# Turning 1/std and a few constants with VectorE and ScalarE instead of TensorE at the start of a layernorm + gated-MLP + state-space kernel

## The chip, the cores and the metric

One core of one Trainium2 chip runs the whole program. The metric is the device time of one execution in microseconds (us). Each profile belongs to one execution and has its own span. The span is about 2 us shorter than the time (before: 502.6 and 504.46 in the profiled execution). A run is in a slow state when its granted TensorE clock is low; that happened once here, to a run of the kernel before (522.75 us at clock 0.949), and that run is in no number below.

## The reference, cut to what matters

```python
# x: 1 x 2048 x 576 in bf16; w_gate, w_up: 576 x 4608; w_down: 4608 x 576
x  = A_x
xn = (x - mean(x)) / sqrt(var(x) + 1e-5)                 # row by row
glu = (sigmoid(xn @ w_gate) * (xn @ w_up)) @ w_down
y   = state_space(xn, Lambda, B, C, log_dt) + xn * Dskip   # a scan over the 2048 rows
out = x + y + glu
```

The kernel takes the rows in blocks of 512. Only the start of the first block matters here. To let TensorE start early, the first ten groups of gate and up columns are multiplied with x that is centred but not yet divided by its standard deviation. Each result is scaled by 1/std afterwards. The matmul leaves the rows of x along the columns of PSUM, while 1/std is computed with one row per partition. So 1/std (4 columns of 128 partitions) must be spread: every partition needs all 512 values along its columns, as the tile `scale0`.

## The kernel before: the parts that the change and the argument touch

```python
class RawGateUp(GateUp):                   # one group of 128 gate and up columns, 512 rows
    def evac(self):
        gu = consts.tile([P, 2, TB], FP32, name="gu", tag=("T2", "C2", "S2")[self.f % 3])
        nc.vector.tensor_mul(gu[:], self.ps[:], scale0[:].unsqueeze(1).to_broadcast([P, 2, TB]))  # VectorE
        sT = evp.tile([P, TB], BF16, name="sT")
        nc.scalar.activation(sT[:], gu[:, 0, :], ACT.Sigmoid)                                     # ScalarE
        h = hpool.tile([P, TB], BF16, name="hT", bufs=2 * FC)
        nc.gpsimd.tensor_mul(h[:], sT[:], gu[:, 1, :])                                            # GpSimd
# ... cut ...
def ln_norm(tt):                           # the next block's first two row tiles, on VectorE
    for dst, src in XN_PARTS:
        nc.vector.tensor_scalar(xn[:, dst], xts[tt][:, src], mvs[nb][:, tl, 0:1], rstds[nb][:, tl:tl + 1],
                                ALU.subtract, ALU.mult)
# ... cut: the start ...
consts_transpose(ptrs[0][:, 0:P])          # two TensorE transposes of 27 rows of constants
ln_log(rstds[0][:], ssq[:, 0:TT_B], 1.0 / D)
ln_exp(0)                                  # 1/std of the first block, on ScalarE
consts_copy(ptrs[0][:, 0:P])               # three ScalarE copies
exp_first()
for tt in range(TT_B, 2 * TT_B - 1):
    ln_stats(tt)                           # VectorE statistics of the next block
for t in range(2):                         # matmuls of the first two groups, rows 256 to 511
    for g in start_groups:
        # ...
        g.turn(t, slice(2 * P, TB))
spread = ptrs[1][:].bitcast(FP32)
for tt in range(TT_B):                     # four TensorE transposes of a broadcast column
    over_rows(spread[:, tt * P:(tt + 1) * P], rstds[0][:, tt:tt + 1])
nc.scalar.copy(scale0[:], spread)
# ... means, squares and 1/std of the next block, load of the sigmoid table (ScalarE) ...
third = RawGateUp(0, 2, 0)
# ...
for g in start_groups:
    g.evac()
```

`gu` has three buffers, so the fourth `gu` waits for the first product on GpSimd. The groups share four PSUM pairs (`pgu`), so a group's first matmul waits for the `gu` of the group four places ahead. A group's stretch of matmuls is called its turn below.

## Time and profile before

| | before |
|---|---|
| time, median of 3 | 504.34 us (504.28 to 504.44) |
| span of the profiled run | 502.6 us |
| TensorE busy | 498.2 us (99%) |
| VectorE, ScalarE, GpSimd busy | 327.0, 213.7, 101.0 us |

### The profile page before, as it was taken

How to read it: one execution, taken by the hardware profiler on the slowest of the kernel's cores; microseconds unless marked ns; L12 is line 12 of the kernel's file. 1: busy time of each engine (PE TensorE's matmuls, PEld its weight loads, DVE VectorE, ACT ScalarE, POOL GpSimd, SP SyncE). 2: the span in 40 equal slices, each digit the busy share in tenths (PEclk: the TensorE clock that was granted, in tenths of full speed). 3: DMA queues.
4: the chain of work that ended last, by engine and by line, in shares of the span. 5: the costliest groups of instructions: out<-in, count | busy, mean ns of one | idle time of the engine just before them, and what ended most of it. 6: DMA issues, size and time to landing. Idle time of an engine off the chain costs nothing.

```text
span 502.6 us, 13289 instructions
## 1 busy us (share of the span) xinstructions
PE 498.2 (99%) x5819; PEld 287.9 (57%) x5819; DVE 327.0 (65%) x717; ACT 213.7 (43%) x395; POOL 101.0 (20%) x140
## 2 busy tenths in 40 slices
PE   8999999999999999999999999999999999999997
PEld 5444675444576444577655445764445774446775
DVE  6969799787794777868769766947666842221112
ACT  6965692555501755610152564015565005553000
POOL 8576100223100133110001332000431101300000
PEclk9999999999999999999999999999999999999999
DMA  9948530244443194221302541100641100500001
GB/s 260 170 103 256 142 58 27 66 137 132 90 103 84 22 262 120 64 76 36 69 2 90 161 132 43 44 25 1 202 121 54 44 26 14 188 1 3 25 26 47
DMA packets 38347, 44.32 MB, mean 88 GB/s; under 512 B 25298, under 2 KB 30866, under 8 KB 38290
## 3 DMA queue, kind: packets, MB, share of 16 engines
q0 software_dynamic: 9424, 32.57, 21.7%
q1 hardware_dynamic: 27906, 10.41, 10.0%
q8 instruction: 45, 0.74, 0.6%
q10 hardware_dynamic: 960, 0.51, 0.4%
q14 instruction: 12, 0.10, 0.1%
HBM read 35.54 MB, written 2.36 MB: 75 GB/s over the span
## 4 chain that ended last, share of the span: by engine, by line
PE 98%; DMA 1%; DVE 0%; issue 0%
PE pgu L565 56%; PE pd L739 33%; PE pbu L565 7%; PE pd L699 1%; PE pd L707 1%; DMA xt<-in_A_x_dram 1%; PE ptr L923 0%; DVE xn L287 0%; DVE xn L933 0%; PE ptr L926 0%; DVE xT L938 0%; DVE ob L708 0%; PE ptr L234 0%
## 5 line engine op out<-in xcount | busy, mean ns | idle before, releaser
L565 PE MATMUL pgu<-xT,wgu 64*128 64x512 bf16 (+1 forms) x2190 | 276.7, 373 | 0.4 <-DVE xT L938 0.4
L565 PEld LDWEIGHTS <-wgu 64*128 64x128 bf16 x2190 | 113.1, 94 | 131.8 <-issue 0.7
L600 ACT ACTIVATE sT<-pgu 128x512 bf16<-128x512 f32 x134 | 80.1, 598 | 159.0 <-PE pgu L565 158.9
L739 PE MATMUL pd<-wd,hT 64*128 64x288 bf16 x2208 | 140.0, 283 | 0.0
L603 DVE TENSOR_TENSOR hT<-sT,uT 128x512 bf16<-128x512 bf16 x134 | 56.8, 424 | 117.7 <-ACT uT L601 117.4
L739 PEld LDWEIGHTS <-hT 64*128 64x128 bf16 x2208 | 107.5, 94 | 30.0
L565 PE MATMUL pgu<-xT,wrem 64*128 64x512 bf16 (+1 forms) x438 | 109.4, 373 | 0.0
L601 ACT CAST uT<-pgu 128x512 bf16<-128x512 f32 x134 | 77.8, 581 | 0.0
L168 POOL DMA_DIRECT2D wgu<-in_B_w_gate_dram x35 | 26.8, 766 | 227.5 <-PE pgu L565 226.1
L182 POOL DMA_DIRECT2D wd<-in_B_w_down_dram x36 | 25.5, 711 | 96.5 <-PE pd L739 96.0
L650 ACT COPY bure<-pbu 128x512 f32<-128x512 f32 x16 | 9.4, 587 | 74.7 <-PE pbu L565 73.9
L565 PEld LDWEIGHTS <-wrem 64*128 64x128 bf16 x438 | 28.0, 94 | 16.9
L757 DVE TENSOR_TENSOR acc<-acc,pd 128x576 f32<-128x576 f32 x36 | 25.4, 747 | 13.0 <-PE pd L739 13.0
L565 PE MATMUL pbu<-xT,bt 64*128 64x512 bf16 x240 | 31.8, 376 | 0.0
L739 PE MATMUL pd<-ctre,hst 64*128 64x288 bf16 x224 | 28.6, 283 | 0.0
L739 PE MATMUL pd<-ctim,hst 64*128 64x288 bf16 x224 | 28.6, 283 | 0.0
L739 PEld LDWEIGHTS <-hst 64*128 64x128 bf16 x504 | 24.5, 94 | 6.7
L168 POOL DMA_DIRECT2D wgu<-in_B_w_up_dram x35 | 26.2, 750 | 0.7 <-issue 0.6
L513 DVE TENSOR_TENSOR_SCAN gre<-r,g0re,wrim 128x512 bf16<-128x512 f32 x20 | 25.6, 1279 | 0.1
L754 DVE TENSOR_TENSOR ob<-acc,pd 128x576 bf16<-128x576 f32 x14 | 9.9, 750 | 23.2 <-PE pd L739 23.2
L565 PEld LDWEIGHTS <-bt 64*128 64x128 bf16 x240 | 12.4, 94 | 14.6
L520 DVE TENSOR_TENSOR_SCAN gim<-r,g0im,wrim 128x512 bf16<-128x512 f32 x16 | 20.3, 1266 | 0.0
(156 smaller groups left out, 369.7 us busy)
## 6 DMA issues: line engine op xcount, KB each, us to landing
wd<-in_B_w_down_dram POOLq DMA_DIRECT2D x36, 288.0 KB, 4.4
wgu<-in_B_w_gate_dram POOLq DMA_DIRECT2D x35, 256.0 KB, 3.5
wgu<-in_B_w_up_dram POOLq DMA_DIRECT2D x35, 256.0 KB, 4.0
out_dram<-ob SPq DMA_DIRECT2D x15, 144.0 KB, 1.8
wrem<-in_B_w_gate_dram POOLq DMA_DIRECT2D x5, 384.0 KB, 6.0
xt<-in_A_x_dram SPq DMA_DIRECT2D x13, 144.0 KB, 4.4
wrem<-in_B_w_up_dram POOLq DMA_DIRECT2D x5, 192.0 KB, 5.8
xt<-in_A_x_dram SPq DMA_DIRECT2D x4, 72.0 KB, 3.6
```

The costliest lines, as they stand in the source:

```text
L168: return [engs[gi].dma_start(w[:, gi, :, :], src[0:R0, fs].rearrange("(c p) f -> p c f", p=P)) for gi, src in enumerate((B_w_gate, B_w_up))]
L182: nc.gpsimd.dma_start(wd[:], B_w_down[f0:f0 + FP * P, :].rearrange("(n p) d -> p n d", p=P))
L513: nc.vector.tensor_tensor_scan(gre[:], r_bc, w[:, 0, :], g0re[:, col], ALU.mult, ALU.add)
L520: nc.vector.tensor_tensor_scan(gim[:], r_bc, w[:, 1, :], g0im[:, col], ALU.mult, ALU.add)
L565: m = nc.tensor.matmul(self.ps[:, which, cols], lhsT, rhs, start=start, stop=stop)
L600: nc.scalar.activation(sT[:], self.ps[:, 0, :], ACT.Sigmoid)
L601: nc.scalar.copy(uT[:], self.ps[:, 1, :])
L603: nc.vector.tensor_mul(h[:], sT[:], uT[:])
L650: nc.scalar.copy(bre[:], self.ps[:, 0, :])
L739: m = nc.tensor.matmul(pds[k][:, a, 0:DH], lhsT[rows, :], rhs[rows, a * DH:(a + 1) * DH], start=turn == 0 and i == 0, stop=turn == 1 and i ...
L754: nc.vector.tensor_add(halves(ob[:]), halves(acc[:]), pd[:, :, 0:DH])
L757: nc.vector.tensor_add(halves(acc[:]), halves(acc[:]), pd[:, :, 0:DH])
```

## The change

The intent is to take six small transposes off TensorE, which has no idle time. VectorE can transpose blocks of 32x32. A transpose of the four columns of 1/std, each broadcast over 32 columns, gives four tiles of 32 partitions (quarters), each right for its own quarter's rows. Each piece must then be copied to the other quarters. Four copies of a quarter go to VectorE and four to ScalarE, and then each engine does one copy of a half. The constants too go through VectorE's transpose, one 32x32 block into each quarter. The order changes with it: the spread sits behind two of the three statistics on VectorE, and the constants' copies sit behind the spread on ScalarE.

```diff
-    def consts_transpose(ps):
-        for half in (slice(0, H), slice(H, P)):
-            nc.tensor.transpose(ps[half, 0:3 * NH], crows[:], ident[0:3 * NH, 0:3 * NH])
+    def consts_transpose():
+        for q in range(4):
+            nc.vector.transpose(crowsT[q * Q:(q + 1) * Q, :], crows[:, q % 2 * Q:(q % 2 + 1) * Q])
 ... cut: consts_copy reads crowsT, crows is padded to 32 rows with zeros, ident32 goes ...
-    def over_rows(dst, col):
-        nc.tensor.transpose(dst, col.to_broadcast([P, P]), ident32[:])
+    def over_rows(dst, src):
+        blocks = ssmp.tile([P, TT_B, Q], FP32, name="blocks", tag="wrim", bufs=1)
+        nc.vector.transpose(blocks[:], src.unsqueeze(2).to_broadcast([P, TT_B, Q]))
+        dst = dst.rearrange("p (t q i) -> p t q i", t=TT_B, i=Q)
+        copies = (nc.vector.tensor_copy, nc.scalar.copy)
+        for i in range(2):
+            for side, copy in enumerate(copies):
+                for j in range(2):
+                    a, b = 2 * side + i, 2 * side + j
+                    copy(dst[b * Q:(b + 1) * Q, :, a, :], blocks[a * Q:(a + 1) * Q, :, :])
+        for side, copy in enumerate(copies):
+            a, b = side * H, (1 - side) * H
+            copy(dst[b:b + H, :, 2 * side:2 * side + 2, :], dst[a:a + H, :, 2 * side:2 * side + 2, :])
 ... cut ...
-    consts_transpose(ptrs[0][:, 0:P])
+    consts_transpose()
     ln_log(rstds[0][:], ssq[:, 0:TT_B], 1.0 / D)
     ln_exp(0)
-    consts_copy(ptrs[0][:, 0:P])
+    for tt in range(TT_B, 2 * TT_B - 2):
+        ln_stats(tt)
+    over_rows(scale0[:], rstds[0][:])
+    ln_stats(2 * TT_B - 2)
+    consts_copy()
     exp_first()
-    for tt in range(TT_B, 2 * TT_B - 1):
-        ln_stats(tt)
 ... cut: the matmuls of the first two groups, as before ...
-    for tt in range(TT_B):
-        over_rows(spread[:, tt * P:(tt + 1) * P], rstds[0][:, tt:tt + 1])
-    nc.scalar.copy(scale0[:], spread)
```

More of the change, by code (lines that the diff above doesn't have):

```diff
@@ L191 @@
     make_identity(nc, ident[:])
-    crows = consts.tile([3 * NH, H], BF16, name="crows")
+    Q = P // 4
+    crows = consts.tile([Q, H], BF16, name="crows")
+    nc.vector.memset(crows[:], 0.0)
     iota = ssmp.tile([P, TB], FP32, name="iota", tag="buim", bufs=2)
@@ L231, with consts_copy @@
     ldt, lre, lim = (cvals[:, i, :] for i in range(3))
-    def consts_transpose(ps):
-        for half in (slice(0, H), slice(H, P)):
-            nc.tensor.transpose(ps[half, 0:3 * NH], crows[:], ident[0:3 * NH, 0:3 * NH])
-    def consts_copy(ps):
-        rows = ps[:, 0:3 * NH].rearrange("p (i a) -> p i a", a=NH)
+    crowsT = consts.tile([P, Q], BF16, name="crowsT")
+    def consts_transpose():
+        for q in range(4):
+            nc.vector.transpose(crowsT[q * Q:(q + 1) * Q, :], crows[:, q % 2 * Q:(q % 2 + 1) * Q])
+    def consts_copy():
+        rows = crowsT[:, 0:3 * NH].rearrange("p (i a) -> p i a", a=NH)
         nc.scalar.copy(cvals[0:H, :, :], rows[0:H, :, 0:NH:2])
@@ L899 @@
     xT_tile(1)
-    ident32 = ssmp.tile([P, P], FP32, name="ident32", tag="wrim", bufs=1)
-    nc.vector.tensor_copy(ident32[:], ident[:])
     start_groups = [RawGateUp(0, f, 0) for f in range(2)]
@@ L968 @@
         rstds[nb] = lnp.tile([P, TT_B], FP32, name="rstd")
-    consts_transpose(ptrs[0][:, 0:P])
+    consts_transpose()
     ln_log(rstds[0][:], ssq[:, 0:TT_B], 1.0 / D)
     ln_exp(0)
-    consts_copy(ptrs[0][:, 0:P])
+    for tt in range(TT_B, 2 * TT_B - 2):
+        ln_stats(tt)
+    scale0 = hpool.tile([P, TB], FP32, name="scale0", tag="hst", bufs=10)
+    over_rows(scale0[:], rstds[0][:])
+    ln_stats(2 * TT_B - 2)
+    consts_copy()
     exp_first()
-    for tt in range(TT_B, 2 * TT_B - 1):
-        ln_stats(tt)
     for t in range(2):
@@ L980 @@
             g.turn(t, slice(2 * P, TB))
-    spread = ptrs[1][:].bitcast(FP32)
-    for tt in range(TT_B):
-        over_rows(spread[:, tt * P:(tt + 1) * P], rstds[0][:, tt:tt + 1])
-    scale0 = hpool.tile([P, TB], FP32, name="scale0", tag="hst", bufs=10)
-    nc.scalar.copy(scale0[:], spread)
     start_mean(2 * TT_B - 1, nc.scalar)
```

## The prediction

> **What bounds the kernel now.** I read the page's part 4 first, then the chain of waits in order of time, then the timeline of the first 36 us for one engine after another, because the diff touches only the start. Part 4 gives the whole chain to TensorE:
>
> ```profile
> PE 98%; DMA 1%; DVE 0%; issue 0%
> ```
>
> So a microsecond taken out of TensorE's own sequence is a microsecond of the result, and work on another engine costs nothing unless TensorE comes to wait for it. The chain in order of time shows the two pieces that the change removes, ptr L234 (constants turned) and ptr L926 (1/std spread); columns are start, length, what:
>
> ```profile
> 9.59 0.13 PE ptr L234 x2
> 9.72 2.07 PE pgu L565 x36
> 11.79 0.58 PE ptr L926 x4
> 12.37 41.98 PE pgu L565 x388
> ```
>
> They are 0.13 + 0.58 = 0.71 us on the path, with no gap around them: the next piece starts where the last ends. From 12.37 on TensorE runs without a wait, so what matters is by how much each matmul group could still afford a late operand. A group's PSUM pair comes free when VectorE has scaled the group four places earlier (gu, L615). VectorE, start and length:
>
> ```profile
> 9.08 0.49 DVE L938 COPY xT<-ptr 128x640 bf16<-128x640 bf16 x1 [0.35 <-PE ptr L923]
> 9.49 0.81 DVE L265 BATCH_NORM_STATS2 bnst<-xt 128x6 f32<-128x288 bf16 x2
> ...
> 11.39 0.77 DVE L265 BATCH_NORM_STATS2 bnst<-xt 128x6 f32<-128x288 bf16 x2
> ...
> 13.02 2.36 DVE L615 TENSOR_TENSOR gu<-pgu,scale 128x1024 f32<-128x1024 f32 x2 [0.62 <-ACT scale L985]
> ...
> 18.40 2.36 DVE L615 TENSOR_TENSOR gu<-pgu,scale 128x1024 f32<-128x1024 f32 x2 [0.40 <-POOL hT L619]
> ```
>
> ```profile
> 27.07 2.35 DVE L615 TENSOR_TENSOR gu<-pgu,scale 128x1024 f32<-128x1024 f32 x2
> ```
>
> and TensorE's two turns that need the first and the eighth of these:
>
> ```profile
> 15.33 1.03 PE L565 MATMUL pgu<-xT,wgu 64*128 64x512 bf16 x8
> ```
>
> ```profile
> 28.93 1.03 PE L565 MATMUL pgu<-xT,wgu 64*128 64x512 bf16 x8
> ```
>
> The reader is to see two things. VectorE is nearly full from 13 to 30.5 us (4.96 us busy of 5 in 20 to 25 and in 25 to 30, in the table by stretches), so a late start there isn't made up. And the slack is small: one gu takes 1.22 us, so the first is done at 13.02 + 1.22 = 14.24 and TensorE wants its PSUM at 15.33 (slack 1.09); the eighth is done at 27.07 + 1.22 = 28.29 and is wanted at 28.93 (slack 0.64). In between I count 1.2 (sixth group of that ring, 18.01 against 19.22), 1.0 (24.08 against 25.05) and more for the others. The tightest place is at 28.93.
>
> ScalarE and GpSimd close the loop, since gu has three buffers and the fourth gu waits for the first product on GpSimd:
>
> ```profile
> 12.40 0.58 ACT L985 COPY scale<-ptr 128x512 f32<-128x512 f32 x1 [0.65 <-PE ptr L926]
> 12.89 0.69 ACT L289 ACTIVATE xn<-xt 128x576 bf16<-128x576 bf16 x1
> ...
> 15.19 1.28 ACT L991 ACT_TABLE_LOAD   x1
> ...
> 16.49 1.15 ACT L617 ACTIVATE sT<-gu 128x512 bf16<-128x512 f32 x2
> ...
> 17.20 3.41 POOL L619 TENSOR_TENSOR hT<-sT,gu 128x512 bf16<-128x512 bf16 x3 [3.97 <-ACT sT L617]
> ```
>
> **What the Trainium skill says.** (1) "VectorE: DVE Perf Modes", section "The three transpose paths": VectorE turns 32x32 blocks only, and a 128x128 bf16 block set takes 311 ns. That is why copies between quarters are needed. The trace of before has no such instruction. (2) The same page, section "Two Vector instructions with no wait between them": an instruction that starts in another group of 32 partitions than the last read or write there starts only when all earlier ones are finished. The trace agrees where it can: memsets that stay at partition 0 overlap (0.81, 0.85, 0.87), the one that moves to partition 64 waits for the end of the one before (0.87 + 0.06 = 0.93, start at 0.97), and the one that moves back waits again (1.08):
>
> ```profile
> 0.85 0.06 DVE L222 MEMSET zero_t<- 128x1 f32 x1
> 0.87 0.06 DVE L244 MEMSET sg_pm<- 64x1 f32 x1
> 0.97 0.06 DVE L245 MEMSET sg_pm<- 64x1 f32 x1
> 1.08 0.06 DVE L481 MEMSET g0re<- 128x5 f32 x1
> ```
>
> (3) "ScalarE: Activation LUTs", section "What ACT_TABLE_LOAD costs": an ACTIVATE with immediate scale takes 186 ns + 0.833 ns per element, and back-to-back ones overlap by about 93 ns. The exp of 128x4 took 206 ns here, the formula gives 189: it agrees. (4) "Advanced Engine Details and Errata", section "VectorE Performance Modes": VectorE's second port is shared with GpSimd and they block each other. The trace shows it: a 128x64 product of VectorE (L343) that starts at 21.00 lasts 1.15 us, until the GpSimd product of 20.93 to 22.10 is over.
>
> **The change part by part.**
> Removed from TensorE: 0.71 us, as above. Removed from VectorE: the 0.56 us copy of the identity at 1.34, which lies in idle time (worth 0). Removed from ScalarE: the 0.58 us scale copy. The order of the built kernel shows that TensorE's remaining matmuls keep their order and that the third group then waits for weights alone. Those land at about 10 us (issued at 5.00, 5.0 us) and their remainder rows at 6.30 + 5.2 = 11.5, wanted at 11.66 + 0.86 = 12.5: no new wait for a DMA. The memset of the constants' rows and the waits of three small loads on it fall before 2 us (0).
>
> Added to VectorE, in its order. a) Four 32x32 transposes of the constants, ahead of the statistics, each into another quarter, so by (2) each held, and the statistics held behind them. With the skill's 311 ns for 128 columns, less 96 columns at 0.96 GHz, one is about 0.21 us (an estimate): 4 x 0.21 = 0.85, so the statistics start at 9.49 + 0.85 = 10.34. b) Two statistics as before, 11.39 - 9.49 = 1.90, plus the tail of 0.08: 12.3. 1/std itself is ready at 11.22 (exp, 11.02 + 0.20) and no longer waited for. c) The block transpose, 128 columns: 0.31, to 12.63. d) Four quarter copies of 128 elements, held one after another: about 0.22 us each (an estimate: 64 cycles at two elements a cycle and some 150 fixed, from the skill's page of (1)), 0.88, to 13.5; up to 0.2 more each while GpSimd writes descriptors until 13.23. e) One half copy of 256 elements, 0.29, to 13.8. f) The third statistics, 11.39 to 12.40 before, so 1.0: 14.8. Only then the first gu: 14.8 against 13.02, late by d0 = 1.8 us.
>
> Added to ScalarE: after the blocks at 12.63, four copies of 128 elements at 186 + 107 - 93 = 200 ns a step, the last in full, 0.89, then one of 256 elements that waits for them, 0.40: 13.97 with the hops. Behind it stand now the constants' copies and their exp, which took 11.76 - 11.13 = 0.63 before: 14.6. Only then comes the mean that began at 12.89: dA = 1.7 us late, and with it everything behind it: table load, first sT at 16.49 + 1.7 = 18.2, first hT done at 20.0, fourth gu at 20.1 against 18.40.
>
> So VectorE's delay is d0 = 1.8 for the first three gu and dA = 1.7 from the fourth on (0.4 us of VectorE idle before it is used up). What TensorE makes of it: each turn may start at its old time less 0.71, or when its PSUM is free. At 15.33: 14.24 + 1.8 = 16.04, which is 0.7 later than before. At 28.93: 28.29 + 1.7 + 0.05 for the semaphore = 30.0, which is 1.1 later than before. The largest of these counts, not their sum, since a turn once late is late for all that follow and the later slack grows by it. After 30.5 VectorE is idle for over a microsecond per group (1.69 us before the hT at 32.24), so nothing more is lost. Sum: -0.71 gained, then 1.8 us of waits, net +1.1 at most of the straight sum.
>
> **The rivals.** A. The straight gain: VectorE's small transposes and copies overlap, d0 about 0.8 and dA about 0.9; the waits shrink to about 1.0 and the net is about +0.3 (504.6). The full -0.71 (503.6) needs both delays under 0.0 to 0.4, which the block transpose behind two statistics nearly rules out: it can't start before 11.8. B. A relief by chance: the 128x64 product of (4) is blocked for 1.15 us because it comes 0.07 us after GpSimd's. If it slips ahead, VectorE gets back about 1.1 us before 28.93, and the turn at 15.33 or 19.22 decides: net +0.3 to +0.7 (504.6 to 505.0). C. Contention: descriptor writing holds the quarter copies, d0 grows to 2.3 or more; then the first gu decides, net +1.2 to +1.6 (505.5 to 505.9). D. The late normalised tiles: ScalarE's last of the next block was done at 20.34, its transposing DMA takes 3 to 4 us, wanted at 26.99; 1.7 us later it lands near 26: it speaks against a new wait there.
>
> **Range and chances.** The straight sum says 504.34 + 1.1 = 505.4, A and B lie 0.4 to 0.8 below it, C half a microsecond above; weighed together, 505.1. 8 times in 10 between 504.2 and 505.9. Two per cent would be 10 us, over ten times any term here: within 2% has 0.985, slower 0.01, faster 0.005.
>
> **What would show it.** TensorE without any ptr L234 or L926 piece, the third group at about 11.66; the first gu at about 14.8 and the fourth at 20.1; in the chain of waits, VectorE's gu appearing ahead of TensorE's turns near 16 and near 30, with idle time of TensorE of 1 to 2 us in the first 31 us that the page before doesn't have; after 31 us the same chain as before, shifted. Wrong would be: a first gu before 14 us, or TensorE with no idle behind gu (then the time is 503.6), or the table load not later than 15.9.

## The result, and the profile after

| | before | after |
|---|---|---|
| time, median of 6 | 504.31 us (504.05 to 504.99) | 505.77 us (505.6 to 506.17) |
| span of the profiled run | 502.6 us | 503.6 us |
| TensorE busy | 498.2 us | 497.7 us |
| VectorE busy | 327.0 us | 329.3 us |

The ratio after/before is 1.0028, with a 95% interval of 1.0016 to 1.0041. Such ratios, here and below, divide the mean time of one kernel's fast runs by that of the other's fast runs in the same rounds, so they are not quite the ratio of the medians quoted. The change is within 2%, and inside that it is a clear small loss: 0.28% of 504.3 is 1.4 us.

The share of the whole chain by engine, part 4 of the page of the kernel after, shows where the loss is: VectorE holds 3% of a chain that was TensorE's almost alone.

```profile
PE 96%; DVE 3%; DMA 1%; issue 0%; DVEq 0%
```

The chain of waits of the kernel after, in order of time (start, length, what), near the two turns that the prediction named:

```profile
13.88 0.83 DVE bnst L269 x2
...
14.86 1.19 DVE gu L619
16.05 0.04 issue
16.09 7.96 PE pgu L569 x72
...
28.67 1.23 DVE gu L619
29.90 0.04 issue
29.94 10.09 PE pgu L569 x91
```

No piece of a transpose of constants or of 1/std is on TensorE any more. Instead the first `gu` (14.86) stands ahead of the turn at 16.09, and the eighth `gu` (28.67) stands ahead of the turn at 29.94. TensorE's own list has the wait at the first of them in brackets:

```profile
16.09 1.04 PE L569 MATMUL pgu<-xT,wgu 64*128 64x512 bf16 x8 [1.66 <-DVE gu L619]
```

The bracket counts idle time from the modelled end of the matmul before. By TensorE's pace the turn is due 0.86 us after the last set of seven matmuls begins, which is at 13.38 here. So it was due at 14.24, and the wait is 1.85. VectorE's list of the kernel after, from the constants to the fourth `gu`:

```profile
9.12 0.84 DVE L238 STREAM_TRANSPOSE crowsT<-crows 32x32 bf16<-32x32 bf16 x4
...
11.88 0.26 DVE L929 STREAM_TRANSPOSE blocks<-rstd 128x128 f32<-128x128 f32 x1
12.18 1.36 DVE L936 COPY scale<-blocks 32x128 f32<-32x128 f32 x4
13.57 0.29 DVE L939 COPY scale<-scale 64x256 f32<-64x256 f32 x1
...
14.86 2.31 DVE L619 TENSOR_TENSOR gu<-pgu,scale 128x1024 f32<-128x1024 f32 x2
...
17.41 1.18 DVE L312 TENSOR_SCALAR xn<-xt,mv,rstd 128x512 bf16<-128x512 bf16 x4
...
19.99 2.36 DVE L619 TENSOR_TENSOR gu<-pgu,scale 128x1024 f32<-128x1024 f32 x2 [0.20 <-POOL hT L623]
```

And the chain of ScalarE and GpSimd beside it, that sets the fourth `gu`:

```profile
12.18 1.21 ACT L936 COPY scale<-blocks 32x128 f32<-32x128 f32 x4 [1.21 <-DVE blocks L929]
13.42 0.40 ACT L939 COPY scale<-scale 64x256 f32<-64x256 f32 x1
...
16.78 1.28 ACT L1002 ACT_TABLE_LOAD   x1
18.07 1.15 ACT L621 ACTIVATE sT<-gu 128x512 bf16<-128x512 f32 x2
```

```profile
18.79 3.42 POOL L623 TENSOR_TENSOR hT<-sT,gu 128x512 bf16<-128x512 bf16 x3 [5.28 <-ACT sT L621]
```

Laid beside the lines of the kernel before, the first `gu` is 1.84 us later (13.02 to 14.86). The table load is 1.59 later (15.19 to 16.78), and the fourth `gu` 1.59 later (18.40 to 19.99). The eighth is 1.60 later (27.07 to 28.67), and TensorE's turn behind it is 1.01 later (28.93 to 29.94). The spans differ by the same 1.0.

One correction belongs to this. In the run profiled after, the start itself was 0.36 us earlier than in the one profiled before: the last copy of the centred x begins at 8.72 and not at 9.08. This is no work of the change, as the kernels derived from before or after begin that copy anywhere from 8.58 to 9.08. Counted from that copy, the turn is 21.22 - 19.85 = 1.37 us late, which is the 1.4 of the mean times.

### The profile page after: what moved, and what is told of

The parts are those of the page before. It is cut to its first block, busy times and chain, and to the rows that moved or that the text cites.

```text
span 503.6 us, 13292 instructions
## 1 busy us (share of the span) xinstructions
PE 497.7 (99%) x5813; PEld 334.1 (66%) x5813; DVE 329.3 (65%) x727; ACT 214.8 (43%) x399; POOL 101.1 (20%) x140
## 4 chain that ended last, share of the span: by engine, by line
PE 96%; DVE 3%; DMA 1%; issue 0%; DVEq 0%
PE pgu L569 53%; PE pd L743 33%; PE pbu L569 7%; PE pd L703 1%; PE pd L711 1%; DVE gu L619 1%; DMA xt<-in_A_x_dram 1%; DVE bnst L269 0%; DVE scale L936 0%; DVE tmpxd L347 0%; PE ptr L925 0%; DVE crowsT L238 0%; DVE xn L291 0%; DVE xn L946 0%; DVE xT L951 0%
## 5 line engine op out<-in xcount | busy, mean ns | idle before, releaser
L569 PEld LDWEIGHTS <-wgu 64*128 64x128 bf16 x2190 | 130.0, 94 | 114.6 <-issue 2.9
L743 PEld LDWEIGHTS <-hT 64*128 64x128 bf16 x2208 | 125.9, 94 | 11.6
L569 PE MATMUL pgu<-xT,wrem 64*128 64x512 bf16 (+1 forms) x438 | 111.9, 373 | 0.0
L569 PEld LDWEIGHTS <-wrem 64*128 64x128 bf16 x438 | 30.4, 94 | 14.5
L743 PEld LDWEIGHTS <-hst 64*128 64x128 bf16 x504 | 28.7, 94 | 2.5
L569 PEld LDWEIGHTS <-bt 64*128 64x128 bf16 x240 | 14.3, 94 | 12.5
```

Of the source, the lines that this page charges most:

```text
L569: m = nc.tensor.matmul(self.ps[:, which, cols], lhsT, rhs, start=start, stop=stop)
L743: m = nc.tensor.matmul(pds[k][:, a, 0:DH], lhsT[rows, :], rhs[rows, a * DH:(a + 1) * DH], start=turn == 0 and i == 0, stop=turn == 1 and i ...
```

## The experiments

The theory is the prediction's: two delays (VectorE's own, and that of ScalarE and GpSimd) of which the larger decides at each of TensorE's turns. Its rivals are that the constants alone do it, that contention with GpSimd does it, or that the order of the instructions does it and not the work. The table gives every run. "Before" is the kernel before in the same rounds, on the same chip.

| kernel | median (lowest to highest), us | ratio to before, 95% | spans, us |
|---|---|---|---|
| 1 constants alone | 504.15 (504.11 to 504.37) | 0.9995 [0.9981, 1.0008] | 502.1 to 502.4 |
| 2 ScalarE's constants early | 507.12 (505.66 to 507.64) | 1.0046 [1.0032, 1.0060] | 503.7 to 505.7 |
| 3 statistics ahead | 506.57 (506.41 to 506.93) | 1.0043 [1.0031, 1.0056] | 504.4 to 504.9 |
| 4 spread alone | 505.74 (505.06 to 505.77) | 1.0023 [1.0010, 1.0035] | 503.1 to 503.8 |
| 5 = 4, product later | 504.61 (504.49 to 504.82) | 1.0005 [0.9991, 1.0019] | 502.4 to 502.7 |
| 6 = 2, product later | 505.46 (505.27 to 505.74) | 1.0022 [1.0009, 1.0035] | 503.2 to 503.7 |
| 7 quiet GpSimd | 505.65 (505.40 to 505.99) | 1.0026 [1.0011, 1.0040] | 503.3 to 503.9 |
| 8 one quarter (one run, state unknown) | 505.34 | none | 503.3 |
| 9 = 5 and 7 | 504.35 (504.28 to 505.47) | 1.0006 [0.9993, 1.0018] | 502.1 to 503.3 |
| 10 before, 4 needless statistics | 505.92 (505.15 to 506.92) | 1.0032 [1.0017, 1.0047] | 503.3 to 505.1 |
| 11 before, 6 needless statistics | 506.80 (506.26 to 506.95) | 1.0046 [1.0032, 1.0060] | 504.3 to 505.1 |
| 12 = 10, product later | 504.54 (504.10 to 505.16) | 1.0000 [0.9986, 1.0013] | 502.1 to 503.2 |

All were correct against the reference. For number 8, whose constants are wrong, that only shows that the tolerance doesn't notice them.

### 1. The constants alone

```diff
 (against before)
+    crows = consts.tile([Q, H], BF16, name="crows")      # and a memset
-    consts_transpose(ptrs[0][:, 0:P])     # TensorE
+    consts_transpose()                    # VectorE, four 32x32
 ... 1/std still spread by TensorE, order as before
```

> Only the constants go to VectorE; 1/std is spread by TensorE as before. Theory (a turn of TensorE waits for the latest of its inputs, the largest lateness counts): the four transposes put the first gu at about 13.3 us against 13.0, inside its slack of 1.1, ScalarE is not later; TensorE loses only its 0.13 us piece, so the span is 502.5 against 502.6 and the ratio to before 0.9995 to 1.0000. Rival (added VectorE work on the start's path costs its own length): the span grows by 0.86 - 0.13 = 0.7 to 503.3, ratio 1.0014.

Measured: 504.15, a tie with before (medians 504.15 and 504.45). TensorE has no wait, and the first `gu` starts at 12.99 although the statistics begin 0.84 us of transposes later: the delay is used up in VectorE's idle time ahead of the first `gu`. So alone this part is neither the loss nor much of a gain. With the spread behind it on VectorE that is no longer so: runs 5 and 6 compare the two.

### 2. ScalarE's copies of the constants ahead of the spread

```diff
 (against after)
     ln_exp(0)
+    consts_copy()
+    exp_first()
     for tt in range(TT_B, 2 * TT_B - 2):
 ...
     ln_stats(2 * TT_B - 2)
-    consts_copy()
-    exp_first()
```

> The changed kernel, but ScalarE does the constants' copies and their exp in its idle 1.2 us ahead of the spread instead of behind it. Theory: the first gu stays at 14.9 and the turn that waits for it at 16.1; the fourth gu comes 0.2 us earlier, the second wait (near 29.9) vanishes as its cause shrinks by up to 0.75; the end moves by the difference of the two latenesses alone, 0.25 us: span 503.35. Rival (ScalarE's chain alone carries the loss): span 603.6 - 0.75, that is 502.85, since the wait near 16 would be made up later. Rival (VectorE's chain alone): span unchanged at 503.6.

(The text has a slip: "603.6 - 0.75" should read 503.6 - 0.75.) This missed. It was not faster than the kernel after but slower and more scattered, with spans from 503.7 to 505.7. The profiled run, the fastest of the five, shows one reason in VectorE's list, where the bracket is a wait for a load of x:

```profile
10.69 0.82 DVE L269 BATCH_NORM_STATS2 bnst<-xt 128x6 f32<-128x288 bf16 x2 [0.35 <-DMA xt<-in_A_x_dram]
```

The start of that run is also 0.36 us later than in the kernel after (copy of centred x at 9.08), so that the first `gu` began at 15.19 and TensorE's turn at 16.42. Its span (503.7) is that of the kernel after. The second wait is gone, as expected (30.01 is 1.94 after the turn before it, the pace), but the late data and the later start hid the gain. The four slower runs have no trace. What they could be came out in run 4, and run 6 tested it. Run 4 shows a collision of VectorE's four normalising instructions with GpSimd's first product. In this profile the two already touch: the normalisation ends at 18.92, and the product starts at 18.86.

### 3. The third statistics ahead of the spread

```diff
 (against after)
-    for tt in range(TT_B, 2 * TT_B - 2):
+    for tt in range(TT_B, 2 * TT_B - 1):
         ln_stats(tt)
     scale0 = ...
     over_rows(scale0[:], rstds[0][:])
-    ln_stats(2 * TT_B - 2)
```

> The changed kernel with the third statistics ahead of the spread instead of behind it: the same VectorE work before the first gu, but ScalarE gets the blocks 0.93 us later. Theory: first gu still at 14.7 to 14.9 and its turn at about 16.0, but the table load, the first hT and the fourth gu 0.9 later, so the second wait grows to put that turn at 30.8 instead of 29.9: span 504.5. Rival (only the first gu counts): span 503.6, no change.

This run separates the two delays. VectorE reaches the first `gu` as early as in the kernel after (14.78, of which 0.40 us is a wait for ScalarE's half copy), but ScalarE's copies come 0.9 us later, and so do the table load (17.71 instead of 16.78) and the fourth `gu` (20.91 instead of 19.99). In TensorE's list:

```profile
16.05 1.04 PE L569 MATMUL pgu<-xT,wgu 64*128 64x512 bf16 x8 [1.63 <-DVE gu L619]
...
30.86 1.04 PE L569 MATMUL pgu<-xT,wgu 64*128 64x512 bf16 x8
```

The first turn is where it was (16.09 after), but the turn near 30 moved from 29.94 to 30.86, by 0.92 us, and the spans rose by 0.8. So ScalarE's delay decides at the late turn, as the prediction says, and the order of the spread in front of the third statistics is worth 0.9 us.

### 4. The spread alone

```diff
 (against the kernel of run 2)
-    consts_transpose()
+    consts_transpose(ptrs[0][:, 0:P])     # TensorE again, 0.13 us
```

> Only the spread goes to VectorE; the constants are turned by TensorE as before and copied by ScalarE in its idle time ahead of the spread. Theory: without the four transposes the first gu starts at about 14.0, its turn at 15.2 to 15.3 (15.33 before); ScalarE's mean begins near 12.95 (12.89 before), so no second wait: span 502.4 to 502.6, ratio 0.9995 to 1.0005. Rival (the spread's own 2 us on VectorE carry the loss, the constants are harmless): span 503.3 or more.

This missed too: 502.5 was expected, and 503.1 to 503.8 came, the number of the rival. Three engines of this run, VectorE, then GpSimd, then TensorE, show a cost that the prediction did not have:

```profile
16.98 2.02 DVE L309 TENSOR_SCALAR xn<-xt,mv,rstd 128x512 bf16<-128x512 bf16 x4
```

```profile
17.79 2.32 POOL L620 TENSOR_TENSOR hT<-sT,gu 128x512 bf16<-128x512 bf16 x2 [3.62 <-ACT sT L618]
```

```profile
20.27 1.04 PE L566 MATMUL pgu<-xT,wgu 64*128 64x512 bf16 x8 [0.54 <-DVE gu L616]
```

The four normalising instructions took 2.02 us instead of the 1.18 of both main kernels, and TensorE waited a second time, at 20.27. The last of the four starts at 17.85, 0.06 us after GpSimd's first product, and lasts 1.16 us, about as long as one product. In the kernel before, the normalisation is over at 16.80 and the first product starts at 17.20. In the kernel after, the figures are 18.59 and 18.79. Here ScalarE is only 0.58 us behind before (sT at 17.07), but VectorE is 1.4 behind (first `gu` at 14.43; 0.53 of it is a load of x that came late), so the product overtakes the normalisation. The Trainium skill has the reason, on "SBUF — State Buffer", section "Who interferes with whom": VectorE and GpSimd share one pair of ports, and the one that has it locks the other out. The 1.16 us agrees with it, and run 5 tests it.

### 5. Run 4 with GpSimd's first product behind the normalisation

```diff
 (against run 4)
         sT = ...; nc.scalar.activation(sT[:], gu[:, 0, :], ACT.Sigmoid)
+        if self.f >= 2: self.product()        # the first two products are issued later
 ...
     for _ in range(2):
         ln_norm(...); ln_dma_transpose(...)
+    for g in start_groups:
+        m = g.product()
+        tc.add_manual_dep(m.ins, last_norm[0].ins.name, PE_ORDER, reason="behind the normalisation")
```

> Only the spread on VectorE (as the run before of that kind, span 503.7 where 502.5 was expected), and GpSimd's first product waits until VectorE's four normalising instructions are done. In that earlier run they took 2.02 us instead of 1.18, as GpSimd's product began at 17.79 amid them, and a second wait of TensorE appeared at 20.27. Theory (ScalarE, now earlier, starts GpSimd inside VectorE's two-port work): the four take 1.2 us again, the wait at 20.3 is gone, only the one near 15.5 stays: span 502.6 to 503.1. Rival (the third gu is late for another cause): the span stays at 503.5 to 503.8.

As expected. VectorE, GpSimd and TensorE of this run:

```profile
16.26 1.18 DVE L311 TENSOR_SCALAR xn<-xt,mv,rstd 128x512 bf16<-128x512 bf16 x4
```

```profile
17.59 4.91 POOL L627 TENSOR_TENSOR hT<-sT,gu 128x512 bf16<-128x512 bf16 x4 [4.25 <-DVE nmr L319]
```

```profile
14.94 1.04 PE L568 MATMUL pgu<-xT,wgu 64*128 64x512 bf16 x8 [0.56 <-DVE gu L618]
```

The normalisation is back at 1.18 us, and the wait near 20 is gone. Counted by TensorE's pace, as for the kernel after, what stays is 0.75 us at 14.94 (the bracket says 0.56) and 0.22 us at 28.75, too short for a bracket, against the 0.58 us of transposes saved. All five spans (502.4 to 502.7) lie below all five of run 4, so it isn't the late load of run 4's profile alone. The time ties with before (504.61 against 504.27). So the spread on VectorE and ScalarE costs about what it saves, within that interval, once the collision is out of the way.

### 6. Run 2 with the same dependence

```diff
 (against run 2: the same edit as in run 5)
```

> ScalarE's constants ahead of the spread (whose runs spread from 503.7 to 505.7 in span) with the same dependence of GpSimd's first product. Theory (the slow ones of those runs are such collisions): all runs within 503.1 to 504.0 in span, median time near 505.5. Rival (the slow ones come from the next block's x landing late, 10.67 in the profiled run): the runs spread as before, up to 505 and more.

As expected: spans of 503.2 to 503.7 instead of 503.7 to 505.7. The scatter of run 2 went when the collision was ruled out. That its slow runs were collisions is therefore likely but not shown: no trace of one exists, and run 6 ran on another chip, where loads of x may have landed otherwise. TensorE's turn near 16 waited, and the one at 29.75 came 0.20 us behind the pace:

```profile
15.95 1.04 PE L571 MATMUL pgu<-xT,wgu 64*128 64x512 bf16 x8 [1.67 <-DVE gu L621]
```

At 505.46 it is 0.3 us below the kernel after (505.77), as expected, but the two intervals overlap widely.

Runs 5 and 6, in the same rounds, differ only in the engine that turns the constants. With VectorE (run 6) the kernel is 0.85 us slower (505.46 against 504.61, and the two sets of times don't overlap), its first `gu` starts at 14.72 instead of 13.71 and the turn behind it at 15.95 instead of 14.94. So the four transposes, free alone (run 1), cost about their own length once the spread stands behind them on VectorE.

### 7. GpSimd quiet during the copies

```diff
 (against after)
-        nc.gpsimd.dma_start(dskip_rows[:], ...)          # after the load of weights (0, 3)
-        load_wgu((0, 4))
+    def last_loads(behind):                              # called behind VectorE's half copy
+        load = nc.gpsimd.dma_start(dskip_rows[:], ...)
+        tc.add_manual_dep(load.ins, behind.ins.name, PE_ORDER, reason="behind the spread")
+        load_wgu((0, 4))
```

> The changed kernel, but GpSimd writes the descriptors of the last two loads of the start (0.55, 0.75 and 0.75 us from 11.45 to 13.5 in the changed kernel) only after VectorE's half copy. Theory: VectorE's four quarter copies take 0.9 us instead of 1.36, the first gu comes at about 14.4 instead of 14.86 and its turn at 15.6 instead of 16.1; but the second wait hangs on ScalarE's chain and stays at 29.9, so the span stays at 503.4 to 503.6. Rival (the copies are slow by themselves): four copies still 1.3 us or more.

This is rival C of the prediction taken alone. VectorE's copies, then TensorE's late turn, in this run:

```profile
12.11 0.90 DVE L939 COPY scale<-blocks 32x128 f32<-32x128 f32 x4
```

```profile
29.88 1.04 PE L572 MATMUL pgu<-xT,wgu 64*128 64x512 bf16 x8 [0.16 <-DVE gu L622]
```

The four copies took 0.90 us, not 1.36, so contention with GpSimd's descriptors was real and cost VectorE 0.46 us in the profiled run. It doesn't strike every time: in run 5 the four took 0.90 us too, though descriptors were being written beside them (11.30 to 12.59). The first `gu` came at 14.35 and the first turn at 15.58, half a microsecond earlier than after (14.86 and 16.09). Yet the turn near 30 is at 29.88 against 29.94, and the time is the same (505.65 against 505.77). The gain at the first turn was given back in two waits (by the pace 0.38 at 25.66 and 0.34 at 29.88, where the kernel after has none and 0.26), because ScalarE's chain, which the edit leaves alone, still sets the fourth `gu` (19.93, waiting 0.65 for GpSimd). This shows what bounds the changed kernel: VectorE's slow copies don't set its end.

### 8. The four constants' transposes into one quarter

```diff
 (against after; the constants come out wrong, on purpose)
-            nc.vector.transpose(crowsT[q * Q:(q + 1) * Q, :], crows[:, ...])
+            nc.vector.transpose(crowsT[0:Q, q * Q:(q + 1) * Q], crows[:, ...])
```

> The changed kernel with the four 32x32 transposes of the constants all written into the first quarter of the partitions, beside one another (wrong constants on purpose). If each is held because it writes to another quarter than the one before: the four take 0.3 to 0.4 us instead of 0.84. If a transpose takes 0.2 us anyway: 0.84 as before.

In VectorE's list:

```profile
9.29 0.47 DVE L239 STREAM_TRANSPOSE crowsT<-crows 32x32 bf16<-32x32 bf16 x4
```

The same four instructions that all start in the first quarter take 0.47 us instead of 0.84, and the statistics behind them start 0.40 us after the first of them instead of 0.86. This is the rule from which the prediction took its 0.85: an instruction that moves to another quarter is held until the ones ahead are done.

### 9. Both cures together

```diff
 (run 5 and the edit of run 7)
```

> The spread alone on VectorE, GpSimd's first product behind the normalisation, and GpSimd's last descriptors behind the spread: the best version that the runs so far point to. In the earlier run of the first two (span 502.4) the half copy took 0.54 us under GpSimd's descriptors and the turn near 14.9 waited 0.56. Theory: half copy 0.29, that wait 0.2 to 0.4, no second wait, span 502.0 to 502.3, ratio to before 0.9990 to 1.0000. Rival: a wait near 18.5 takes its place, span 502.4 or more.

This is the best version with the spread off TensorE. The half copy took 0.29 us and the first wait is 0.34 by its bracket, as expected. By the pace TensorE waits 0.50 us at 14.64 and 0.21 at 28.45, for 0.58 us saved. Three of the five spans lie in the expected 502.0 to 502.3. Its profiled span of 502.1 equals the fastest of before, but its five runs reach up to 503.3, and the median ties with before: 504.35 against 504.34. So nothing here beats the kernel before; it only takes back the loss of the kernel after.

### 10 and 11. The kernel before with VectorE delayed

```diff
 (against before, 4 in run 10, 6 in run 11)
+    idle = consts.tile([P, 4, BN], FP32, name="idle")
+    for i in range(4):
+        nc.vector.bn_stats(idle[:, i, :], xts[0][:, 0:DH])    # read by nobody
     spread = ptrs[1][:].bitcast(FP32)
```

These delay VectorE alone, without the change, to see whether its slack of 1.09 us at 15.33 is what the prediction says.

> The kernel before with four needless statistics (4 x 0.39 us) on VectorE ahead of its first gu, nothing else: 0.62 us of it fall into idle time, the first gu is 0.9 us late, under the slack of 1.1. Theory of slack: no wait of TensorE, span as before (502.2 to 502.9). Rival (each us of VectorE there costs a us): span 503.3.

> The kernel before with six needless statistics ahead of the first gu: 1.7 us late, above the slack of 1.1. Theory of slack: TensorE's turn at 15.33 comes at about 16.0, one wait of 0.6 to 0.7, span 502.9 to 503.3. Rival (VectorE's delay is made up by its later idle time): span as before.

Run 10 missed: no change was expected and 1.6 us came. Yet the slack was there. Counted from the last copy of centred x, the first `gu` was 1.18 us late (a load of x had held the statistics for 0.35), and the turn behind it came only 0.13 behind the pace (14.96 instead of 14.83). But VectorE, GpSimd and TensorE show the collision again, in a kernel that has no part of the change:

```profile
16.28 2.87 DVE L308 TENSOR_SCALAR xn<-xt,mv,rstd 128x512 bf16<-128x512 bf16 x4
```

```profile
16.70 2.40 POOL L619 TENSOR_TENSOR hT<-sT,gu 128x512 bf16<-128x512 bf16 x2 [2.49 <-ACT sT L617]
```

```profile
20.41 1.04 PE L565 MATMUL pgu<-xT,wgu 64*128 64x512 bf16 x8 [1.39 <-DVE gu L615]
```

The normalisation met both products and took 2.87 us. Run 11 has both costs. The first turn waited 1.25 us at 16.42, where 0.6 to 0.7 was expected, because a load of x held VectorE's statistics for 0.92 us. By the same count the first `gu` was 2.46 us late and the turn 1.42, so here as in run 10 about 1.05 us of lateness was free, near the slack of 1.09 that the prediction read. A second wait of 1.10 at 21.58 came on top, behind a normalisation of 2.12 us. That put run 11 above its expectation.

### 12. Run 10 with the product behind the normalisation

```diff
 (run 10 and the edit of run 5)
```

> The kernel before with the four needless statistics (first gu 0.9 us late), and GpSimd's first product behind VectorE's normalisation. Without that dependence the same lateness gave a span of 503.9: the first gu's turn didn't wait, but VectorE's normalisation, now later against ScalarE, met GpSimd's products and took 2.87 us instead of 1.18, and the turn at 20.41 waited. Theory (the slack at the first gu is 1.1 and the loss was the collision): normalisation 1.2 us, no wait of TensorE, span 502.1 to 502.8. Rival (VectorE's lateness itself): the wait near 20 stays and the span is 503.3 or more.

As expected in the median: 504.54 against 504.51 of before. The needless work is still there, the normalisation is back, and no wait stands near 20:

```profile
17.04 1.18 DVE L310 TENSOR_SCALAR xn<-xt,mv,rstd 128x512 bf16<-128x512 bf16 x4
```

Two of the five spans (502.9 and 503.2) lie above the expected 502.8. The profiled run is the slowest. In it loads of x held VectorE's statistics for 0.66 and 0.28 us (the later one landed at 12.06), and the turn waited 0.52 us at 15.72, which is no part of the edit.

## Why the prediction was right, point by point

The time (505.77 against 505.1, range 504.2 to 505.9) is inside the range, 0.13 below its upper end, and the class is the one given 0.985. The forecast of 505.1 was a loss of 0.8 us, and 1.4 came: the mechanism was right, its sizes were short. By its own steps:

- **TensorE's 0.71 us.** They are gone: no such piece is on TensorE, and the third group starts at 11.22. The predicted 11.66 was 0.44 off, of which 0.36 is the early start of that run.
- **The constants' transposes, 0.85.** Measured 0.86 from the first to the statistics behind, and run 8 confirms the cause, the change of quarter. Alone (run 1) they cost nothing. Ahead of the spread they cost about their length (run 6 against run 5, 0.85 us), and the prediction was right to count them into d0.
- **The block transpose, 0.31.** Measured 0.26.
- **The four quarter copies, 0.88 plus contention.** Measured 1.36, and 0.90 without the descriptors (run 7). The bare term was right; "up to 0.2 more each" was given without a source, and it was too little for one of the four, which took 0.52.
- **The first gu at 14.8.** Measured 14.86, but from the earlier start. Counted from the last copy of centred x, the first `gu` is 6.14 - 3.94 = 2.20 us late instead of 1.8. The size that was off is the contention in the copies, 0.46.
- **ScalarE's chain, 1.7 late.** The table load and the first sT are 1.6 later in the two traces and 1.94 counted from the same copy (9.35 against 7.41). The mis-sized term is the four copies at "a step of 200 ns": they took 1.21 us, not 0.89, because none overlaps the one before.
- **TensorE's waits.** The turns came at 16.09 and 29.94 where 16.04 and 30.0 stood, and no other waits lie between or after. The waits are 1.85 and 29.94 - 29.68 = 0.26 (the turn before stands at 27.74, and the pace is 1.94 from turn to turn). Together 2.11, less 0.71, gives 1.40: the measured 1.4. That both turns agree to 0.06 us is partly luck, as this run began 0.36 us early. Counted from the last copy of centred x, they are 0.41 and 0.30 later than predicted.
- **"The largest of these counts, not their sum."** Runs 3 and 7 show it. In 3 only ScalarE's chain was moved, and the end moved by 0.92. In 7 only VectorE's part was made faster, and the end stayed.
- **The rivals.** A (overlap, 504.6) did not occur: the transposes and copies are held one by one. B (relief by chance) did not occur either: the residual products of VectorE took 1.49 and 1.24 us per pair after, against 1.48 and 1.24 before, since all of that stretch moved by the same 1.6 us. C was real on VectorE, but did not reach the end (run 7). D was right: no wait for a transposing load appears.
- **The number.** The straight sum (+1.1, so 505.4) was nearer than 505.1. What drew it down was the weight given to A and B, and neither happened. The straight sum itself lacked 0.3 to 0.4, the ScalarE copies and the contention.

What the prediction did not have at all is the collision of the normalisation with GpSimd's first products. The changed kernel escapes it in its profiled run, as VectorE and ScalarE are late by nearly the same amount (1.84 and 1.59) and the normalisation ends 0.2 us ahead of the product. It appears as soon as one is late and the other is not: with the spread alone (run 4), and with VectorE alone delayed (runs 10 and 11). Read by TensorE's slack alone, run 10 is free, and that is what its expectation said.

What stays open: the slow runs of run 2's kernel have no trace, so the collision there is inferred from run 6. The scatter of run 9's time is not explained. It may be late loads of x, as in runs 2 and 12, but no trace shows it.

## What to carry to other kernels

When work is taken off the engine that bounds a kernel, compare its few tenths of a microsecond with the slack of each chain that receives it, and look at the latest turn, not only the first: here 0.71 us were saved and 2.11 us of waits came. Delays of two engines that feed the same place don't add up, so making the wrong one faster (run 7) gains nothing, and the order of a new piece in a queue can weigh as much as its work (0.92 us in run 3). A piece that costs nothing alone can cost its whole length once more work stands behind it (the constants: nothing in run 1, 0.85 us between runs 5 and 6). When one engine is delayed, check also which instructions of a partner with a shared port it will now meet: run 10's 1.6 us came from a collision, not from the slack.

## What the Trainium skill lacked or had wrong

- "VectorE: DVE Perf Modes", section "The three transpose paths", has no time for a small or an fp32 transpose. Here one fp32 block transpose of 128x128 elements took 0.26 us, and a held 32x32 bf16 one about 0.21 us (0.84 for four in four quarters, 0.47 for four in one quarter). The rule of the same page on holding agrees, but the page puts no price on it.
- "ScalarE: Activation LUTs", section "What ACT_TABLE_LOAD costs", says that back-to-back instructions overlap by about 93 ns. Four copies of 32x128 between quarters took 1.21 us with no overlap (in run 7's chain one takes 0.29 or 0.30, as the page's formula gives, and the next starts after its end). With the overlap it would be 0.89. Each of the four writes to another quarter than the one before. Of ScalarE's three copies of the constants in the kernel before, the second moves to the other half and starts at 11.29, after the first ended (11.28), while the third stays there and starts at 11.36, 0.10 before the second ends. So the overlap may hang on staying in the same quarter. No run here tests that.
- "SBUF — State Buffer", section "Who interferes with whom", says that whichever of VectorE and GpSimd issues first blocks the other, but for descriptors it has only the one case, VectorE delaying those that GpSimd writes. Run 7 shows the reverse: the descriptors delayed VectorE's fp32 copies, 1.36 us against 0.90. Not every copy beside a descriptor was slow (run 5); in the kernel after, the two slow ones ended 0.03 and 0.04 us after the end of a descriptor instruction.
- No page of those read gives the scatter of loads at the start of a kernel. VectorE's statistics waited for a load of x in the profiles of runs 2, 4, 10, 11 and 12 (0.35, 0.53, 0.35, 0.92 and 0.66 us), and not in those of the other runs.
